# Causal attention with decay and a SiLU feed-forward: score matmuls of two heads in one step, the mask moved from TensorE to VectorE, buffers regrouped

## The chip, the cores and the metric

The kernel runs on one core of a Trainium2 chip. The metric is the device time of one execution in microseconds; the time before is the median of five runs. A core has five engines that work side by side: TensorE (PE; its weight loads are shown apart as PEld), VectorE (DVE), ScalarE (ACT), GpSimd (POOL) and SyncE (SP, which here only issues transfers). Each runs its own instructions strictly in the order in which they were compiled and waits for others by semaphores. Matmuls write to PSUM, which has eight banks of 2 KB per partition; all else lies in SBUF.

## The reference

Eight batches of eight heads, 576 tokens, head size 64; then a feed-forward from 512 to 2048 and back over all 4608 tokens.

```python
scores = scale * np.matmul(q, k.transpose(0, 1, 3, 2))
cum = np.cumsum(np.log(np.clip(f, 0.0001, 1.0)), axis=-1)
scores = np.where(causal, -1e9, scores + cum[..., :, None] - cum[..., None, :])
attn = softmax(scores)                 # over the keys
x = heads_side_by_side(attn @ v)       # (4608, 512)
h = x @ w_in
out = (h * sigmoid(h)) @ w_out         # (4608, 512)
```

## The kernel before

The program is written in Tile: it emits instructions in the order of the Python code, and a scheduler at compile time orders each engine's instructions by that order as priority, taking a later one where an earlier one isn't ready in its own model of time. Buffers come from pools; `bufs` is how many tiles of a tag may live at once, and a tile's slot is given on when its last reader is done.

**A head** (64 in all, `bh` = batch x 8 + head) goes through these steps. The 576 tokens are five blocks, four of 128 and one of 64.

- `load_head` (L155): SP issues three loads (q, k, v) into a staging tile; the last 64 tokens of all heads of a batch come in one load each (`load_tails`, L135) and POOL copies them in.
- `stage_prep` (L173): DVE casts q and k side by side to bf16 (L186, L187), POOL casts v and sets a column of ones beside it (L190 to L197), PE transposes the five blocks into one PSUM tile `tpqk` (L201), DVE copies that to `qkT` (L205): q transposed in partitions 0 to 63, k transposed in 64 to 127. SP then moves k's half to partitions 0 to 63 of `kT` by a transfer (L207), because both operands of a score matmul must lie in the same partitions.
- `stage_scores` (L210): for each block of keys, transposed scores (keys on partitions, queries at or after the block as columns): matmuls of at most 512 columns into `sc` (L223), which is one PSUM bank with two buffers. For the diagonal block a second matmul adds -30000 where the key comes after the query (L232: `tneg` against the identity). ACT takes the exponential with the decay as a bias per partition into `uT` (L239). That is six score matmuls, five mask matmuls and six exponentials a head: 448 + 128, 448, 320, 192 and 64 columns.
- `stage_av` (L258): for each block of queries PE multiplies `uT` by v with its column of ones (L268, fifteen matmuls a head) into one PSUM tile `av` (two buffers); DVE takes the reciprocal of the sums and multiplies (L278, L279; L288, L289 for the last 64 tokens) into `y`.

**A batch** ends with `stage_xT` (L295): twenty transposes through a PSUM tile `tpx` (pool `ptr`, one buffer), copied by DVE (L307) into `xT`.

**The feed-forward** works on nine groups of 512 tokens. `moe_m1` (L316): for each of 16 blocks of the hidden size four matmuls into `hp` (L323), then ACT's tanh (L331) and a gating multiply on DVE that reads `hp` again (L334). `moe_m2` (L344): for each of four blocks of tokens sixteen matmuls into `po` (L352), a scaled copy by ACT (L360) and a store issued by POOL (L363). `hp` and `po` share two PSUM buffers. After a batch m1 of the group that it completes is emitted, then m2 of the group before (`maybe_emit_moe_after_batch`, L378). As later heads come later in the program, they fill the gaps of m1 and run alone when m2 is done. After the last batch two groups' m1 and three groups' m2 are left, with no heads beside them but those at the beginning.

Loads are emitted four heads ahead and preparations two heads ahead (L391, L392). The PSUM banks: `tpqk` 1, `sc` 2, `av` 2, `tpx` 1, `hp` and `po` 2.

Of the kernel before, what the change touches and what calls it, by code (L numbers as in the profile page):

```python
# [8 lines left out]

ACT = mybir.ActivationFunctionType  # L10
ALU = mybir.AluOpType
FP32 = mybir.dt.float32
BF16 = mybir.dt.bfloat16
P = 128

MASK_ON_PE = True


@with_exitstack
def kernel(  # L20
# [46 lines left out]
    if MASK_ON_PE:  # L67
        tneg = const.tile([P, P], BF16, name="tneg")
        make_upper_triangular(nc, tneg, val=-30000.0, diag=False)
    else:  # L70
# [56 lines left out]
    psc = ctx.enter_context(tc.tile_pool(name="psc", bufs=2, space=bass.MemoryType.PSUM))  # L127
    pav = ctx.enter_context(tc.tile_pool(name="pav", bufs=2, space=bass.MemoryType.PSUM))
    ptr = ctx.enter_context(tc.tile_pool(name="ptr", bufs=1, space=bass.MemoryType.PSUM))
    php = ctx.enter_context(tc.tile_pool(name="php", bufs=2, space=bass.MemoryType.PSUM))  # L130

    stg: dict[int, tuple] = {}
# [37 lines left out]
        )  # L170
        stg[bh] = (qkf, vf)

    def stage_prep(bh):  # L173
        b, h = divmod(bh, H)
        qkf, vf = stg[bh]
        if HAS_TAIL:
            qt, kt, vt = tails[b]
            nc.gpsimd.tensor_copy(out=qkf[:NT_TAIL, NB - 1, 0:D], in_=qt[:NT_TAIL, h, :])
            nc.gpsimd.tensor_copy(
                out=qkf[:NT_TAIL, NB - 1, D : 2 * D], in_=kt[:NT_TAIL, h, :]  # L180
            )
            nc.gpsimd.tensor_copy(out=vf[:NT_TAIL, NB - 1, :], in_=vt[:NT_TAIL, h, :])
        qk_bf = conv.tile([P, NB, 2 * D], BF16, name="qk_bf", tag="qk_bf")
        v_bf = conv.tile([P, NB, D + 1], BF16, name="v_bf", tag="v_bf")
        if HAS_TAIL:
            nc.vector.tensor_copy(out=qk_bf[:, 0 : NB - 1, :], in_=qkf[:, 0 : NB - 1, :])  # L186
            nc.vector.tensor_copy(  # L187
                out=qk_bf[:NT_TAIL, NB - 1, :], in_=qkf[:NT_TAIL, NB - 1, :]
            )
            nc.gpsimd.tensor_copy(out=v_bf[:, 0 : NB - 1, 0:D], in_=vf[:, 0 : NB - 1, :])  # L190
            nc.gpsimd.tensor_copy(
                out=v_bf[:NT_TAIL, NB - 1, 0:D], in_=vf[:NT_TAIL, NB - 1, :]
            )
        else:
            nc.vector.tensor_copy(out=qk_bf[:, :, :], in_=qkf[:, :, :])
            nc.gpsimd.tensor_copy(out=v_bf[:, :, 0:D], in_=vf[:, :, :])
        nc.gpsimd.memset(v_bf[:, :, D : D + 1], 1.0)  # L197
        tp = ptp.tile([P, S], BF16, name="tpqk", tag="tpqk")
        for c in range(NB):
            n = bs[c]  # L200
            nc.tensor.transpose(  # L201
                tp[:, c * P : c * P + n], qk_bf[:n, c, :], ident_bf[:n, :n]
            )
        qkT = qktp.tile([P, S], BF16, name="qkT", tag="qkT")
        nc.vector.tensor_copy(out=qkT[:, :], in_=tp[:, :])  # L205
        kT = qktp.tile([P, S], BF16, name="kT", tag="kT")
        nc.sync.dma_start(out=kT[0:D, :], in_=qkT[D : 2 * D, :])  # L207
        return (qkT[0:D, :], kT[0:D, :], v_bf)

    def stage_scores(bh, prepped):  # L210
        b, h = divmod(bh, H)
        qT, kT, v_bf = prepped
        u = upool.tile([P, UW], BF16, name="uT", tag="uT")
        for kb in range(NB):
            nk = bs[kb]
            q0 = kb * P
            nqtot = S - q0
            col = 0
            first = True
            while col < nqtot:  # L220
                ncols = min(448 if (nqtot - col) > 512 else 512, nqtot - col)
                sc = psc.tile([P, 512], FP32, name="sc", tag="sc")
                nc.tensor.matmul(  # L223
                    sc[:nk, 0:ncols],
                    lhsT=kT[:, q0 : q0 + nk],
                    rhs=qT[:, q0 + col : q0 + col + ncols],
                    start=True,
                    stop=(not (first and MASK_ON_PE)),
                )
                if first and MASK_ON_PE:  # L230
                    nq0 = nk
                    nc.tensor.matmul(  # L232
                        sc[:nk, 0:nq0],
                        lhsT=tneg[:nq0, 0:nk],
                        rhs=ident_bf[:nq0, :nq0],
                        start=False,
                        stop=True,
                    )
                nc.scalar.activation(  # L239
                    out=u[:nk, uoff[kb] + col : uoff[kb] + col + ncols],  # L240
                    in_=sc[:nk, 0:ncols],
                    func=ACT.Exp,
                    bias=negcumT[:nk, kb, bh : bh + 1],
                    scale=scale,
                )
                if first and not MASK_ON_PE:
                    nq0 = nk
                    nc.vector.tensor_tensor(
                        out=u[:nk, uoff[kb] : uoff[kb] + nq0],
                        in0=u[:nk, uoff[kb] : uoff[kb] + nq0],  # L250
                        in1=mask01[:nk, :nq0],
                        op=ALU.mult,
                    )
                col += ncols
                first = False
        return (u, v_bf)

    def stage_av(bh, scored):  # L258
        b, h = divmod(bh, H)
# [53 lines left out]
    NG = (NT + TG - 1) // TG  # L313
    gstate: dict[int, tuple] = {}

    def moe_m1(g):  # L316
        t0 = g * TG
        ntg = min(TG, NT - t0)
        gte = gpool.tile([P, NFC, TG], BF16, name="gtile", tag="gtile")
        for fc in range(NFC):  # L320
            hp = php.tile([P, TG], FP32, name="hp", tag="hp")
            for cc in range(NCC):
                nc.tensor.matmul(  # L323
                    hp[:, :ntg],
# [19 lines left out]
    def moe_m2(g):  # L344
# [2 lines left out]
        nb_tok = (ntg + P - 1) // P  # L347
        for tb in range(nb_tok):
            ntb = min(P, ntg - tb * P)
            po = php.tile([P, TG], FP32, name="po", tag="hp")  # L350
            for fc in range(NFC):
                nc.tensor.matmul(  # L352
                    po[:ntb, :DM],
# [34 lines left out]
    ytiles: dict[int, bass.AP] = {}  # L388
    prepped: dict[int, tuple] = {}

    LOAD_AHEAD = 4  # L391
    PREP_AHEAD = 2  # L392

    load_tails(0)
# [5 lines left out]
    ytiles[0] = ypool.tile([P, NB, DM], BF16, name="y", tag="y")  # L400
    for bh in range(min(PREP_AHEAD, BH)):
        pb, _ = divmod(bh, H)
        if pb not in ytiles:
            ytiles[pb] = ypool.tile([P, NB, DM], BF16, name="y", tag="y")
        prepped[bh] = stage_prep(bh)

    for bh in range(BH):
        b, h = divmod(bh, H)
        if b not in ytiles:
            ytiles[b] = ypool.tile([P, NB, DM], BF16, name="y", tag="y")  # L410
        scored = stage_scores(bh, prepped[bh])
        lt = bh + LOAD_AHEAD
        if lt < BH:
            lb, lh = divmod(lt, H)
            if lh == 0 and lb not in tails:
                load_tails(lb)
            load_head(lt)
        nxt = bh + PREP_AHEAD
        if nxt < BH:
            nb2, nh2 = divmod(nxt, H)  # L420
            if nb2 not in ytiles:
                ytiles[nb2] = ypool.tile([P, NB, DM], BF16, name="y", tag="y")
            prepped[nxt] = stage_prep(nxt)
        stage_av(bh, scored)
        if h == H - 1:
            stage_xT(b)
            maybe_emit_moe_after_batch(b)

    for g in range(NG):
        if g not in gstate:  # L430
# [36 lines left out]
```

## Time and profile before

| what | us |
|---|---|
| median of five runs | 608.18 |
| lowest, highest | 607.56, 610.42 |
| the profiled execution | 607.63 |
| its span, first to last instruction | 605.5 |
| mean granted TensorE clock over the span | 0.874 of full |

The costliest kinds of work, by busy time in the span: m1's matmuls 158.7, m2's 125.6, the score matmuls 131.7, the mask matmuls 80.5, the av matmuls 97.5 us on PE; the exponentials 170.7 and tanh 86.1 on ACT; the gating multiply 98.7 on DVE. How to read such lines: an instruction is named by its line in the kernel, its engine, its operation, what it writes and reads, and its shape; behind the bar stand its busy time in all, the mean of one in ns, then how long the engine stood idle before such instructions and what ended that. Matmuls overlap in time, so the sum of their durations exceeds the time that they hold PE; their start times tell what each one costs.

### The profile page before, as it was taken

Reading aid. Unit: us, or ns where it says so; the run is one execution under the profiler, and the core shown is the slowest. Engines: PE = TensorE matmul, PEld = TensorE weight load, DVE = VectorE, ACT = ScalarE, POOL = GpSimd, SP = SyncE. Lnnn points to the kernel's source line nnn. Section 1 sums busy time; section 2 is a strip of 40 time slices with the busy share of each in tenths; the row PEclk is TensorE's granted clock in tenths of the full one; section 3 lists DMA queues with packets and bytes.
Section 4 is the critical chain, followed back from the end, with each engine's and each line's share of the span. In section 5 each row is a group of like instructions: output and inputs, shape, how many; then the busy total and the mean of one; then the engine's idle time right before and its main releaser. Section 6 shows DMA issues by size and latency. Waiting matters only on the chain.

```text
span 605.5 us, 9158 instructions
## 1 busy us (share of the span) xinstructions
PE 548.0 (90%) x3301; PEld 262.3 (43%) x3301; DVE 233.5 (39%) x634; ACT 275.1 (45%) x572; POOL 102.1 (17%) x432
## 2 busy tenths in 40 slices
PE   0039999999999999999999999999999998888896
PEld 0015554454445444544454445544454444333342
DVE  1033345644604461546244633454245502532400
ACT  1025545655626472647354734564355535333311
POOL 2032221222122111311031112100110010001011
PEclk9999999957996699759985998599858995899999
DMA  8993443634674412441243034200100020001011
GB/s 169 204 171 77 102 102 80 144 71 111 154 171 116 105 41 75 121 109 38 61 125 88 19 78 116 51 15 28 62 16 6 11 74 6 1 14 57 1 69 70
DMA packets 124765, 47.41 MB, mean 78 GB/s; under 512 B 115696, under 2 KB 121840, under 8 KB 124720
## 3 DMA queue, kind: packets, MB, share of 16 engines
q1 hardware_dynamic: 119248, 33.20, 25.6%
q0 software_dynamic: 5472, 13.63, 7.9%
q8 instruction: 26, 0.43, 0.3%
q14 instruction: 19, 0.16, 0.1%
HBM read 36.85 MB, written 9.44 MB: 76 GB/s over the span
## 4 chain that ended last, share of the span: by engine, by line
PE 73%; issue 16%; SPq 5%; ACT 2%; DMA 1%; POOL 1%; DVE 1%; POOLq 0%; ACTq 0%; DVEq 0%
PE hp L323 18%; PE sc L223 16%; PE po L352 14%; PE av L268 10%; PE sc L232 7%; PE tpqk L201 5%; PE tpx L302 3%; SPq L163 2%; ACT uT L239 2%; SPq L167 1%; SPq L159 1%; POOL out_dram L363 1%; DMA qkf<-in_k_dram 1%; DMA kT<-qkT 1%; ACT L239 0%
## 5 line engine op out<-in xcount | busy, mean ns | idle before, releaser
L239 ACT ACTIVATE uT<-sc,negcumT 128x448 bf16<-128x448 f32 (+4 forms) x384 | 170.7, 480 | 91.8 <-PE sc L232 88.9
L323 PE MATMUL hp<-xT,w_in_bf 128*128 128x512 bf16 x576 | 158.7, 402 | 6.3 <-DVE gtile L334 5.4
L223 PE MATMUL sc<-qkT,kT 64*128 64x448 bf16 (+4 forms) x384 | 131.7, 346 | 10.1 <-ACT uT L239 6.2
L334 DVE SCALAR_TENSOR_TENSOR gtile<-th,hp 128x512 bf16<-128x512 bf16 x144 | 98.7, 686 | 74.4 <-ACT th L331 73.5
L331 ACT ACTIVATE th<-hp 128x512 bf16<-128x512 f32 x144 | 86.1, 598 | 90.9 <-PE hp L323 73.3
L352 PE MATMUL po<-w_out_bf,gtile 128*128 128x512 bf16 x576 | 125.6, 379 | 0.8 <-DVE gtile L334 0.8
L268 PE MATMUL av<-v_bf,uT 128*128 128x65 bf16 (+2 forms) x960 | 97.5, 225 | 0.1
L352 PEld LDWEIGHTS <-gtile 128*128 128x128 bf16 x576 | 56.0, 98 | 67.7 <-issue 1.3
L268 PEld LDWEIGHTS <-uT 128*128 128x128 bf16 (+2 forms) x960 | 66.8, 118 | 34.0 <-issue 20.2
L232 PE MATMUL sc<-ident_bf,tneg 128*128 128x128 bf16 (+1 forms) x320 | 80.5, 252 | 0.0
L323 PEld LDWEIGHTS <-w_in_bf 128*128 128x128 bf16 x576 | 50.9, 102 | 61.0 <-issue 23.2
L205 DVE COPY qkT<-tpqk 128x576 bf16<-128x576 bf16 x64 | 29.2, 456 | 115.9 <-PE tpqk L201 46.8
L190 POOL CAST v_bf<-vf 128x256 bf16<-128x256 f32 x64 | 25.5, 399 | 269.1 <-PE av L268 154.5
L201 PE MATMUL tpqk<-ident_bf,qk_bf 128*128 128x128 bf16 (+1 forms) x320 | 45.3, 256 | 26.4 <-DVE qk_bf L186 18.4
L360 ACT ACTIVATE osb<-po 128x512 f32<-128x512 f32 x36 | 21.5, 597 | 104.3 <-PE po L352 104.3
L223 PEld LDWEIGHTS <-kT 64*128 64x128 bf16 (+1 forms) x384 | 37.9, 101 | 54.6 <-issue 30.8
L232 PEld LDWEIGHTS <-tneg 128*128 128x128 bf16 (+1 forms) x320 | 34.5, 108 | 57.2 <-issue 47.2
L363 POOL DMA_DIRECT2D out_dram<-osb x36 | 19.5, 542 | 167.5 <-ACT osb L360 164.6
L201 PEld LDWEIGHTS <-qk_bf 128*128 128x128 bf16 (+1 forms) x320 | 26.1, 112 | 41.7 <-DVE qk_bf L186 18.6
L186 DVE CAST qk_bf<-qkf 128x512 bf16<-128x512 f32 x64 | 27.2, 424 | 39.1 <-DMA qkf<-in_k_dram 27.8
L278 DVE RECIPROCAL rec<-av 128x4 f32<-128x4 f32 x64 | 11.7, 183 | 77.2 <-PE av L268 76.3
L279 DVE TENSOR_TENSOR y<-av,rec 128x256 bf16<-128x256 f32 x64 | 27.1, 424 | 2.0
(31 smaller groups left out, 177.4 us busy)
## 6 DMA issues: line engine op xcount, KB each, us to landing
out_dram<-osb POOLq DMA_DIRECT2D x36, 256.0 KB, 2.3
qkf<-in_q_dram SPq DMA_DIRECT2D x64, 128.0 KB, 2.8
qkf<-in_k_dram SPq DMA_DIRECT2D x64, 128.0 KB, 2.9
vf<-in_v_dram SPq DMA_DIRECT2D x64, 128.0 KB, 2.5
kT<-qkT SPq DMA_DIRECT2D x64, 72.0 KB, 2.0
w_in_bf<-in_moe_w_in_dram POOLq DMA_DIRECT2D x1, 2048.0 KB, 13.8
w_out_bf<-in_moe_w_out_dram POOLq DMA_DIRECT2D x1, 2048.0 KB, 26.1
qt<-in_q_dram SPq DMA_DIRECT2D x8, 128.0 KB, 3.2
```

The lines of the kernel that those rows point to most:

```text
L186: nc.vector.tensor_copy(out=qk_bf[:, 0 : NB - 1, :], in_=qkf[:, 0 : NB - 1, :])
L201: nc.tensor.transpose(tp[:, c * P : c * P + n], qk_bf[:n, c, :], ident_bf[:n, :n])
L205: nc.vector.tensor_copy(out=qkT[:, :], in_=tp[:, :])
L223: nc.tensor.matmul(sc[:nk, 0:ncols], lhsT=kT[:, q0 : q0 + nk], rhs=qT[:, q0 + col : q0 + col + ncols], start=True, stop=(not (first and MA ...
L232: nc.tensor.matmul(sc[:nk, 0:nq0], lhsT=tneg[:nq0, 0:nk], rhs=ident_bf[:nq0, :nq0], start=False, stop=True,)
L239: nc.scalar.activation(out=u[:nk, uoff[kb] + col : uoff[kb] + col + ncols], in_=sc[:nk, 0:ncols], func=ACT.Exp, bias=negcumT[:nk, kb, bh : ...
L268: nc.tensor.matmul(av[:nq, qb, :], lhsT=u[:nk, loff : loff + nq], rhs=v_bf[:nk, kb, 0 : D + 1], start=(kb == 0), stop=(kb == qb),)
L279: nc.vector.tensor_tensor(out=y[:, 0:nfull, h * D : (h + 1) * D], in0=av[:, 0:nfull, 0:D], in1=rec[:, 0:nfull, None].to_broadcast([P, nful ...
L323: nc.tensor.matmul(hp[:, :ntg], lhsT=w_in_bf[:, cc, fc * P : (fc + 1) * P], rhs=xT[:, cc, t0 : t0 + ntg], start=(cc == 0), stop=(cc == NCC ...
L331: nc.scalar.activation(out=th[:, :ntg], in_=hp[:, :ntg], func=ACT.Tanh, scale=0.5)
L334: nc.vector.scalar_tensor_tensor(out=gte[:, fc, :ntg], in0=th[:, :ntg], scalar=1.0, in1=hp[:, :ntg], op0=ALU.add, op1=ALU.mult,)
L352: nc.tensor.matmul(po[:ntb, :DM], lhsT=gte[:, fc, tb * P : tb * P + ntb], rhs=w_out_bf[:, fc, :], start=(fc == 0), stop=(fc == NFC - 1),)
```

## The change

Scores are computed for two heads at once (`PAIR_SCORES`). Of a pair, the even head has q and k in partitions 0 to 63 as before; for the odd head the transfer moves q up, so that q and k lie in partitions 64 to 127. A tile `sc` now has two banks (still two buffers), one bank per head; the two score matmuls are emitted one behind the other under `tc.high_priority()`, which gives them the priority of the program's start. Then come the two heads' exponentials.

The mask matmul is gone. After the exponential of a diagonal block DVE overwrites with zeros what lies below the diagonal of that transposed block, where the key comes after the query (`copy_predicated` with a mask of int16).

To make room in PSUM, `av` has one buffer in place of two and `tpx` takes its slot from the same tag. The pools `conv`, `qktp` and `upool` grow by one, `stage` shrinks from 12 to 10. Loads are emitted six heads ahead, preparations one pair ahead. After the last head, every second output tile of m1 and m2 takes a slot of `sc`, so that four buffers take turns in place of two.

```diff
-MASK_ON_PE = True
+MASK_MODE = "pred"
+PAIR_SCORES = True
...
+        mask_lo = const.tile([P, P], mybir.dt.int16, name="mask_lo")
+        make_lower_triangular(nc, mask_lo, val=1.0, diag=False)
+        zeros = const.tile([P, P], BF16, name="zeros")
+        nc.gpsimd.memset(zeros[:, :], 0.0)
...
-    stage = ctx.enter_context(tc.tile_pool(name="stage", bufs=12))
+    stage = ctx.enter_context(tc.tile_pool(name="stage", bufs=10))
     tailp = ctx.enter_context(tc.tile_pool(name="tailp", bufs=2))
-    conv = ctx.enter_context(tc.tile_pool(name="conv", bufs=3))
-    qktp = ctx.enter_context(tc.tile_pool(name="qktp", bufs=3))
-    upool = ctx.enter_context(tc.tile_pool(name="upool", bufs=2))
+    conv = ctx.enter_context(tc.tile_pool(name="conv", bufs=4))
+    qktp = ctx.enter_context(tc.tile_pool(name="qktp", bufs=4))
+    upool = ctx.enter_context(tc.tile_pool(name="upool", bufs=3))
...
-    pav = ctx.enter_context(tc.tile_pool(name="pav", bufs=2, space=bass.MemoryType.PSUM))
-    ptr = ctx.enter_context(tc.tile_pool(name="ptr", bufs=1, space=bass.MemoryType.PSUM))
+    pav = ctx.enter_context(tc.tile_pool(name="pav", bufs=1, space=bass.MemoryType.PSUM))
...
+        sh = qktp.tile([P, S], BF16, name="shT", tag="shT")
+        if upper:
+            nc.sync.dma_start(out=sh[D : 2 * D, :], in_=qkT[0:D, :])
+            return (sh[D : 2 * D, :], qkT[D : 2 * D, :], v_bf)
+        else:
+            nc.sync.dma_start(out=sh[0:D, :], in_=qkT[D : 2 * D, :])
+            return (qkT[0:D, :], sh[0:D, :], v_bf)
...
+            nc.vector.copy_predicated(
+                out=u[:nk, col_off : col_off + nq0],
+                mask=mask_lo[:nk, :nq0],
+                data=zeros[:nk, :nq0],
+            )
...
+                sc = psc.tile([P, 2, 512], FP32, name="sc", tag="sc")
+                with tc.high_priority():
+                    for i, bh in enumerate(bhs):
+                        qT, kT, v_bf = preps[i]
+                        nc.tensor.matmul(
+                            sc[:nk, i, 0:ncols],
+                            lhsT=kT[:, q0 : q0 + nk],
+                            rhs=qT[:, q0 + col : q0 + col + ncols],
+                            start=True,
+                            stop=(not (first and MASK_MODE == "matmul")),
+                        )
+                for i, bh in enumerate(bhs):
+                    nc.scalar.activation(
+                        out=us[i][:nk, uoff[kb] + col : uoff[kb] + col + ncols],
+                        in_=sc[:nk, i, 0:ncols],
+                        func=ACT.Exp,
+                        bias=negcumT[:nk, kb, bh : bh + 1],
+                        scale=scale,
                     )
...
+                    if first and MASK_MODE != "matmul":
+                        apply_mask(us[i], nk, nk, uoff[kb])
...
-            tp = ptr.tile([P, NCC, P], BF16, name="tpx", tag="tpx")
+            tp = pav.tile([P, NCC, P], BF16, name="tpx", tag="av")
...
+    def moe_psum(nm):
+        if not tailflag[0]:
+            return php.tile([P, TG], FP32, name=nm, tag="hp")
+        tailn[0] += 1
+        if tailn[0] % 2:
+            return php.tile([P, TG], FP32, name=nm, tag="hp")
+        t2 = psc.tile([P, 2, 512], FP32, name="sc", tag="sc")
+        return t2[:, 0, :]
...
+    for gi, grp in enumerate(groups):
+        b0 = grp[0] // H
+        for bh in grp:
+            ensure_y(bh // H)
+        scored = stage_scores(list(grp), [prepped[bh] for bh in grp])
+        for bh in grp:
+            lt = bh + LOAD_AHEAD
...
+        if gi + 1 < len(groups):
+            for bh in groups[gi + 1]:
+                ensure_y(bh // H)
+                prepped[bh] = stage_prep(bh, is_upper(bh))
+        for i, bh in enumerate(grp):
+            b, h = divmod(bh, H)
+            stage_av(bh, scored[i])
+            if h == H - 1:
+                stage_xT(b)
+                tailflag[0] = bh == BH - 1
+                maybe_emit_moe_after_batch(b)
```

More of the change, by code (lines that the diff above doesn't have):

```diff
@@ L7 @@
 from concourse._compat import with_exitstack
-from concourse.masks import make_identity, make_upper_triangular
+from concourse.masks import (
+    make_identity,
+    make_lower_triangular,
+    make_upper_triangular,
+)
 ACT = mybir.ActivationFunctionType
@@ L221, in stage_scores @@
                 ncols = min(448 if (nqtot - col) > 512 else 512, nqtot - col)
[L222 to L237, printed above, removed]
-                    )
@@ L239, in stage_scores @@
[L239 to L253, printed above, removed]
+                sc = psc.tile([P, 2, 512], FP32, name="sc", tag="sc")
@@ L254, in stage_scores @@
                 col += ncols
                 first = False
-        return (u, v_bf)
+        return [(us[i], preps[i][2]) for i in range(len(bhs))]
     def stage_av(bh, scored):
@@ L314 @@
     gstate: dict[int, tuple] = {}
+    tailflag = [False]
+    tailn = [0]
+    def moe_psum(nm):
[6 more added lines that the diff above has]
+        return t2[:, 0, :]
     def moe_m1(g):
@@ L389, with is_upper, ensure_y @@
     prepped: dict[int, tuple] = {}
-    LOAD_AHEAD = 4
-    PREP_AHEAD = 2
-    load_tails(0)
+    LOAD_AHEAD = 6
+    if PAIR_SCORES:
+        groups = [(bh, bh + 1) if bh + 1 < BH else (bh,) for bh in range(0, BH, 2)]
+    else:
+        groups = [(bh,) for bh in range(BH)]
+    def is_upper(bh):
+        return PAIR_SCORES and (bh % 2 == 1)
+    def ensure_y(b):
+        if b not in ytiles:
+            ytiles[b] = ypool.tile([P, NB, DM], BF16, name="y", tag="y")
     for bh in range(min(LOAD_AHEAD, BH)):
```

74 lines of the change are left out of this document (34 added, 40 removed).

## The prediction

> **What bounds the kernel now.** I read the busy times first, then the span by stages, then the order of TensorE's work in one head.
>
> ```profile
> PE 548.0 (90%) x3301; PEld 262.3 (43%) x3301; DVE 233.5 (39%) x634; ACT 275.1 (45%) x572; POOL 102.1 (17%) x432
> ```
>
> TensorE (PE) is the only engine near full; VectorE (DVE) and ScalarE (ACT) are under half. But the span is made of unlike stages, so next come stretches of it (columns: stretch, its length, then busy us and count of instructions for PE, PEld, DVE, ACT and POOL, then the granted clock, DMA share, GB/s):
>
> ```profile
> 42.60:90.00 47.40, 46.60 (x304) 24.47 (x304) 18.09 (x64) 26.40 (x59) 10.90 (x51) 1.00 0.40 89
> 305.40:328.70 23.30, 22.89 (x174) 12.67 (x173) 11.03 (x40) 13.93 (x31) 7.23 (x33) 0.65 0.47 113
> 328.70:333.20 4.50, 4.50 (x22) 1.70 (x20) 1.74 (x4) 0.60 (x1) 0.00 (x0) 0.52 0.33 75
> 328.70:354.00 25.30, 25.30 (x154) 11.17 (x152) 15.61 (x36) 14.71 (x30) 3.20 (x16) 0.92 0.20 46
> 354.00:367.90 13.90, 13.90 (x68) 6.17 (x65) 0.69 (x1) 2.88 (x6) 1.82 (x5) 1.00 0.24 77
> 517.70:538.80 21.10, 18.43 (x79) 7.25 (x77) 11.72 (x19) 9.16 (x16) 0.00 (x0) 0.93 0.00 1
> 552.60:572.10 19.50, 15.41 (x66) 6.17 (x65) 10.32 (x15) 10.05 (x17) 0.54 (x1) 1.00 0.04 14
> ```
>
> The first row is the opening run of heads; the next four are one round, which recurs seven times: attention heads alone (23.3 us), the first MoE product m1 with heads in its gaps (25.3, its first 4.5 shown apart), the second product m2 alone (13.9). The last two rows are m1 in the tail, with no heads left. In the round PE is busy 98 to 100%: every nanosecond of PE work there is on the path. In the last row it is busy 15.41 of 19.50, for 64 matmuls of the size and number that m2 does in 13.9. How many heads a stage holds is the count of L288, once per head (here columns are DVE alone):
>
> ```profile
> 305.40:328.70 23.30, 0.74 (x5) 0.65 0.47 113
> 328.70:354.00 25.30, 0.45 (x3) 0.92 0.20 46
> ```
>
> Five heads take 4.66 us each alone, three hide in m1. Now one head on PE, by start times, at a low clock:
>
> ```profile
> 192.02 0.55 PE L223 MATMUL sc<-qkT,kT 64*128 64x448 bf16 x1
> 192.50 0.26 PE L268 MATMUL av<-v_bf,uT 64*64 64x65 bf16 x1
> 192.69 0.29 PE L232 MATMUL sc<-ident_bf,tneg 128*128 128x128 bf16 x1
> 192.91 0.28 PE L223 MATMUL sc<-qkT,kT 64*128 64x128 bf16 x1
> 193.13 0.77 PE L201 MATMUL tpqk<-ident_bf,qk_bf 128*128 128x128 bf16 x5
> 193.76 0.53 PE L223 MATMUL sc<-qkT,kT 64*128 64x448 bf16 x1
> 194.22 0.29 PE L232 MATMUL sc<-ident_bf,tneg 128*128 128x128 bf16 x1
> 194.45 0.45 PE L223 MATMUL sc<-qkT,kT 64*128 64x320 bf16 x1
> 194.82 0.29 PE L232 MATMUL sc<-ident_bf,tneg 128*128 128x128 bf16 x1
> 194.91 0.32 PE L268 MATMUL av<-v_bf,uT 128*128 128x65 bf16 x2
> 195.24 0.32 PE L223 MATMUL sc<-qkT,kT 64*128 64x192 bf16 x1
> 195.48 0.29 PE L232 MATMUL sc<-ident_bf,tneg 128*128 128x128 bf16 x1
> 195.57 0.37 PE L268 MATMUL av<-v_bf,uT 128*128 128x65 bf16 x3
> 195.87 0.26 PE L223 MATMUL sc<-qkT,kT 64*64 64x64 bf16 x1
> 195.94 0.24 PE L232 MATMUL sc<-ident_bf,tneg 64*64 64x64 bf16 x1
> 196.12 0.82 PE L268 MATMUL av<-v_bf,uT 128*128 128x65 bf16 x9
> 196.87 0.55 PE L223 MATMUL sc<-qkT,kT 64*128 64x448 bf16 x1
> ```
>
> From one 448-column score to the next head's is 4.85 us, without a wait. Durations overlap, so each step is priced by the start of the next. The five masks (L232) take 0.22 + 0.23 + 0.09 + 0.09 + 0.18 = 0.81. A mask that a 64-row score follows takes 0.23; one that a 128-row av matmul follows takes 0.09: part of the price is the change of shape. The six scores (L223) take 0.48 + 0.22 + 0.46 + 0.37 + 0.24 + 0.07 = 1.84.
>
> **The change part by part.** *Masks leave PE:* 0.81 us a head at this clock. At full clock the same pair of steps shows
>
> ```profile
> 371.08 0.23 PE L232 MATMUL sc<-ident_bf,tneg 128*128 128x128 bf16 x1
> 371.24 0.31 PE L223 MATMUL sc<-qkT,kT 64*128 64x320 bf16 x1
> ```
>
> that is 0.16 for 0.23, a ratio of 0.70, so I take 0.57 there.
>
> *Scores in pairs:* head 2k has q and k on rows 0 to 63, head 2k+1 on rows 64 to 127, each with its own PSUM bank. No row shows both halves at once. The pair's steps cost between one head's 1.84 (both halves together) and twice that (one after the other): a saving of 0.92 to 0 a head, at full clock 0.64 to 0. I take the whole saving, since the rows say that a score uses 64 of the rows and the other head's operands lie on the other 64. Less than nothing is excluded: the matmuls are the same and the changes of shape become fewer. The Trainium skill, "TensorEngine Tiling (Array Packing)", Key Properties, says that tiles work independently and that a change of tiling mode drains the engine; the mask rows' 0.23 against 0.09 agree with the drain, and nothing here tests the independence. By its first half alone the forecast below holds; without it the first rival does.
>
> So a head needs 4.85 - 0.81 - 0.92 = 3.1 us of PE at the low clock.
>
> *Masks land on DVE:* five predicated copies a head, 128 or 64 elements a row, inputs in SBUF. None is in the trace. The nearest rows:
>
> ```profile
> L279 DVE TENSOR_TENSOR y<-av,rec 128x256 bf16<-128x256 f32 x64 | 27.1, 424 | 2.0
> L289 DVE TENSOR_SCALAR y<-av,rec 64x64 bf16<-64x64 f32 x64 | 17.4, 272 | 1.1
> L187 DVE CAST qk_bf<-qkf 64x128 bf16<-64x128 f32 x64 | 13.9, 218 | 0.2 <-POOL qkf L179 0.2
> ```
>
> 218 ns is one input of the same length, 424 two inputs at twice the length. I take 0.26, nearer to the first, since length counts for most; 5 x 0.26 = 1.3 us a head, with ends of 1.1 and 2.1. Over 64 heads DVE goes from 233.5 to some 317 us busy. In the lone heads DVE works 11.03 / 5 = 2.2 us a head, then 3.5. ACT is unchanged:
>
> ```profile
> L239 ACT ACTIVATE uT<-sc,negcumT 128x448 bf16<-128x448 f32 (+4 forms) x384 | 170.7, 480 | 91.8 <-PE sc L232 88.9
> ```
>
> six exponentials of 480 ns, 2.9 us a head. So in the lone stretch the order turns round: DVE 3.5, PE 3.1, ACT 2.9. Each mask also waits for its exponential, and the av matmuls of its block for it; what queues behind on DVE is the next heads' casts, the copies to qkT, and in m1 the gating multiply that frees the hp buffers. Three engines so close don't interlock perfectly: I allow DVE 92%, 3.8 us a head (an estimate).
>
> *One av buffer for two, shared with tpx:* the second head's av must wait until DVE has read the first's. The read is L279 and L289 (0.70) with two reciprocals ahead, about 1.0. Cover: PE meanwhile has the next pair's scores, emitted at high priority, and its tpqk transposes. If that cover is gone it is the second rival. The deeper conv, qktp and uT pools hold two heads at once, the 12 to 10 stage buffers still hold six heads ahead: nothing.
>
> *Start:* the first pair needs two transfers (one a head, as before) ahead of its first exponentials of both heads; SP issues them in its queue:
>
> ```profile
> 36.69 0.52 SPq L207 DMA_DIRECT2D kT<-qkT  x1
> 37.26 0.59 SPq L159 DMA_DIRECT2D qkf<-in_q_dram  x1
> 37.95 0.51 SPq L207 DMA_DIRECT2D kT<-qkT  x1
> ```
>
> The second is 1.26 later: +1.3 us, once. Loading six heads ahead in place of four puts no more before them: SP already put loads of a later head between the two. POOL's two more constants are single short operations.
>
> *Tail:* output tiles of m1 and m2 after the last head come from four buffers, not two. The 552.60 stretch should shrink from 19.5 to near m2's 13.9; I take 14.8, -4.7. In the 517.70 stretch I take PE's idle time, 21.10 - 18.43 = 2.7.
>
> *Sum.* Lone heads of a round: 5 x (4.66 - 3.8) = -4.3. m1 stretch: PE loses 3 x (0.57 + 0.64) = 3.6 of 25.3; DVE there is 15.61 + 3 x 1.3 = 19.5 in 21.7, 90%, so I give back 0.8: -2.8. m2 stays. Seven rounds of -7.1: -49.7. The opening stretch, 47.4 us for nine heads, is at the slow pace (its clock is printed 1.00, but 5.3 us a head isn't): 9 x (4.85 - 3.8) = -9.5. Tail -7.4, start +1.3. Together -65.3. The profiled execution took 607.6 (span 605.5 and 2.1 around it), 0.6 under the median: 608.2 - 65.3 = 543 us.
>
> **The rivals.** *The halves don't run together.* Then only the masks are saved: lone heads 0.75 each (between 0.57 and 0.81, clock 0.65), 3.8 a round; m1 3 x 0.57 = 1.7; seven rounds 38.5, opening 9 x 0.81 = 7.3, tail 7.4, start +1.3: 556 us. For it: no row shows two halves at work. Against it: the two write separate banks and read separate rows.
>
> *The single av buffer becomes a chain.* If the next pair's exponentials can't start until the av results of this one are out, a pair takes 2 x 2.9 of exponentials, then the first head's last nine av matmuls (0.75), their reading (1.0), the second head's fifteen (0.33 + 0.30 + 0.75 + 0.19 = 1.6), their reading (1.0): 10.1, or 5.05 a head. Against 4.66 that is +1.9 a round in the lone stretch with nothing gained in m1, opening +1.8, tail -7.4, start +1.3: 608.2 + 9, 617 us. It decides from about 4.8 us a head, where 44 lone heads eat the tail's gain. Against it: uT has three buffers, so one head of the next pair can go on, and nine of fifteen av matmuls need not wait for the end.
>
> *The clock stays low in m1.* The lone heads run at 0.65 and m1 starts at 0.52 over its first 4.5 us, then recovers (0.92 over the stretch). If a PE that idles more never recovers, m1's matmuls take twice 13.9, with three heads of 3.1 some 37 us for 22.5: +14.6 x 7 on 543, 645 us; it turns to a loss from 9 us a round. Against it: 64 long matmuls a stretch stay, and they raised the clock each time. The Trainium skill, "TensorE: Matmul & The Clock Gate", Part 1, says that the clock halves after idle windows and returns after about 3.4 us of sustained work; the 4.5 us above agree.
>
> *Better overlap:* DVE full at 3.3 a head (masks at 218 ns) and m1 losing all 3.6: 10.4 a round, opening 14, tail and start as above: 515 us.
>
> **How the numbers follow.** Forecast, with the better overlap in it, 0.62; halves apart 0.20; av chain 0.10; low clock 0.04; mixed effects that cancel 0.04. A difference under 0.3% (1.8 us) can't be told from none here. Faster 0.84, same 0.04, slower 0.12. The range goes from 512, just under the better overlap, to 575, past the halves-apart case with DVE waits of its own; above lie the chain and the clock.
>
> **What would show it.** Right: PE's busy time near 450, DVE's near 317; two score matmuls of a pair starting within some tens of ns; lone heads at 3.8 with DVE the fullest; predicated copies near 0.26; the last m1 at 14.8. Wrong: predicated copies above 0.42; PE waiting for reciprocals or L289 before av for microseconds; m1 stretches at a clock near 0.5.

## The result and the profile after

The changed kernel takes 529.84 us (median of nine; 526.86 to 531.06) against 608.5 (median of sixteen): a ratio of 0.869, 95% interval 0.868 to 0.871. The forecast was 543 with a range of 512 to 575: faster, and by 13 us more than said. The busy times of the profiled execution (span 526.6 us):

```profile
PE 447.8 (85%) x2981; PEld 220.6 (42%) x2981; DVE 287.5 (55%) x954; ACT 256.6 (49%) x572; POOL 107.9 (20%) x433
```

PE fell by 100 us, to the 450 that was forecast. DVE rose by 54 and not by the 84 that was forecast, though the copies themselves cost what was forecast (below): the durations of all DVE instructions add up to 253 us before and 339 after, 86 more, but busy time counts a moment once where instructions overlap. The same kinds of stretch as before, in the same columns: the opening, one round (heads alone, m1, m2), and the two m1 of the tail:

```profile
44.20:84.90 40.70, 31.68 (x250) 18.17 (x250) 27.75 (x113) 24.87 (x63) 12.62 (x54) 1.00 0.61 134
220.30:235.00 14.70, 11.39 (x116) 7.13 (x116) 12.08 (x52) 9.37 (x24) 6.13 (x25) 0.77 0.62 145
235.00:259.20 24.20, 24.20 (x176) 11.35 (x174) 18.71 (x59) 17.14 (x39) 4.14 (x20) 0.93 0.30 68
259.20:273.50 14.30, 14.30 (x70) 6.33 (x69) 1.55 (x5) 2.39 (x4) 2.03 (x5) 1.00 0.25 80
448.50:465.70 17.20, 17.20 (x79) 7.77 (x78) 11.26 (x19) 8.96 (x15) 0.00 (x0) 0.85 0.00 0
479.40:493.40 14.00, 14.00 (x67) 6.34 (x66) 9.88 (x15) 9.57 (x17) 0.54 (x1) 1.00 0.05 19
```

The heads that end in the lone stretch and in m1, again by one DVE instruction a head (now L309):

```profile
220.30:235.00 14.70, 0.59 (x4) 0.77 0.62 145
235.00:259.20 24.20, 0.60 (x4) 0.93 0.30 68
```

Two things are to be seen. A lone head now takes 14.7 / 4 = 3.7 us in this round (forecast 3.8). And m1, as long as before, holds four heads where it held three, so fewer are left to run alone. The lone stretch shrank from 23.3 to 14.7, twice what I had forecast. In it no engine is full any more: PE 11.4 of 14.7, DVE 12.1.

To compare kernels I cut every span at three places: the first exponential, the beginning of m1 of the first group, and that of m1 of the eighth (the last but one); m1's beginning is taken 1.1 us ahead of the group's first tanh. "Half clock" is the time at which the records grant PE half its clock; the records show only full and half, and none exists for the opening, so it is left out there.

| kernel | median us | until the first exponential | opening | middle | tail | half clock |
|---|---|---|---|---|---|---|
| before | 608.5 | 42.6 | 48.1 | 428.2 | 86.5 | 153 |
| changed | 529.8 | 44.2 | 41.5 | 364.0 | 76.9 | 87 |
| same_half | 545.5 | 44.3 | 45.5 | 377.3 | 75.5 | 95 |
| mask_on_pe | 549.1 | 44.2 | 45.4 | 380.6 | 77.3 | 97 |
| no_prio | 539.4 | 44.3 | 41.5 | 375.1 | 77.2 | 125 |
| tail_two | 540.0 | 43.7 | 41.5 | 365.1 | 87.1 | 90 |
| before_mask_dve | 554.3 | 43.6 | 43.6 | 379.5 | 86.5 | 105 |
| before_tail_four | 599.0 | 43.1 | 48.1 | 429.4 | 75.8 | 160 |
| single_heads | 567.5 | 42.9 | 44.8 | 401.8 | 76.5 | 125 |
| four_undone | 593.5 | 44.2 | 47.9 | 413.3 | 86.5 | 144 |
| before_av_one | 618.1 | 42.7 | 48.2 | 438.4 | 86.5 | 177 |
| mask_pool | 527.3 | 44.3 | 42.8 | 362.7 | 76.4 | 87 |
| late_weights | 522.9 | 22.6 | 57.2 | 365.0 | 76.6 | 91 |
| pool_late | 511.6 | 19.9 | 54.1 | 359.8 | 75.5 | 85 |

One of the four runs of mask_on_pe took 829 us and one of the four of tail_two 803, in a slower state; the medians given include them, and those of the other three runs are 548.9 and 539.9.

In the profiles of all kernels but before, changed and pool_late, 39 to 41 of the 1152 feed-forward matmuls have no record (PE x2940 beside PEld x2981), so PE's busy time there reads about 4 us too low. That is an estimate, with each missing one put in behind its weight load.

Between the first two rows the start costs 1.6, the opening gains 6.6, the middle 64.2 and the tail 9.6: 78.8 us of span. The forecast had, for the same four, a cost of 1.3 and gains of 9.5, 49.7 and 7.4. The surplus lies in the middle. The middle as seven rounds, m1 and m2 each from the first to the last of its weight loads and the lone stretch between m2 and the next m1 ("exps" are exponentials):

| kernel | lone stretches, us | heads that end there | m1, us | heads that end there | exps in m1 | exps in m2 |
|---|---|---|---|---|---|---|
| before | 175.7 | 35 | 165.0 | 18 | 100 | 8 |
| changed | 100.9 | 25 | 171.3 | 29 | 164 | 28 |
| no_prio | 135.3 | 29 | 154.0 | 23 | 101 | 12 |
| before_mask_dve | 123.3 | 27 | 168.7 | 25 | 139 | 5 |
| mask_pool | 109.0 | 28 | 165.2 | 24 | 148 | 12 |

Over all rounds a lone head takes 175.7 / 35 = 5.0 us before and 100.9 / 25 = 4.0 after, so the round shown is one of the shorter ones.

### The profile page after: what moved, and what is told of

It reads as the page before. It is cut to its first block, busy times and chain, and to the rows that moved or that the text cites. A ratio compares the mean times of both kernels' runs of the same rounds, so it can differ in the third digit from the quotient of the medians.

```text
span 526.6 us, 8852 instructions
## 1 busy us (share of the span) xinstructions
PE 447.8 (85%) x2981; PEld 220.6 (42%) x2981; DVE 287.5 (55%) x954; ACT 256.6 (49%) x572; POOL 107.9 (20%) x433
## 4 chain that ended last, share of the span: by engine, by line
PE 57%; issue 20%; SPq 7%; DVE 6%; DMA 4%; ACT 3%; POOL 2%; POOLq 0%; ACTq 0%; DVEq 0%
PE hp L356 20%; PE po L385 13%; PE av L289 9%; PE sc L258 8%; PE tpqk L213 4%; PE tpx L323 3%; SPq L175 3%; ACT uT L266 2%; SPq L179 2%; SPq L171 2%; DMA qkf<-in_k_dram 2%; POOL out_dram L396 2%; DVE qkT L217 1%; DMA shT<-qkT 1%; DVE y L300 1%
## 5 line engine op out<-in xcount | busy, mean ns | idle before, releaser
L266 ACT ACTIVATE uT<-sc,negcumT 128x448 bf16<-128x448 f32 (+4 forms) x384 | 157.2, 490 | 57.7 <-PE sc L258 55.3
L356 PE MATMUL hp<-xT,w_in_bf 128*128 128x512 bf16 x512 | 146.8, 407 | 1.9 <-DVE gtile L367 1.7
L364 ACT ACTIVATE th<-hp 128x512 bf16<-128x512 f32 x128 | 77.2, 603 | 67.0 <-PE hp L356 61.7
L385 PE MATMUL po<-w_out_bf,gtile 128*128 128x512 bf16 x480 | 107.8, 379 | 0.0
L235 DVE COPY_PREDICATED uT<-mask_lo,zeros 128x128 bf16<-128x128 int16 (+1 forms) x320 | 80.1, 273 | 27.4 <-ACT uT L266 24.9
L289 PE MATMUL av<-v_bf,uT 128*128 128x65 bf16 (+2 forms) x960 | 72.7, 209 | 11.1 <-DVE uT L235 7.4
L356 PEld LDWEIGHTS <-w_in_bf 128*128 128x128 bf16 x576 | 51.1, 102 | 57.2 <-issue 16.9
L289 PEld LDWEIGHTS <-uT 128*128 128x128 bf16 (+2 forms) x960 | 54.7, 108 | 46.7 <-issue 14.6
L258 PE MATMUL sc<-qkT,shT 64*128 64x448 bf16 (+1 forms) x192 | 55.5, 328 | 7.8 <-ACT uT L266 5.7
L258 PE MATMUL sc<-shT,qkT 64*128 64x448 bf16 (+2 forms) x192 | 56.2, 337 | 2.9 <-DMA shT<-qkT 2.9
L258 PEld LDWEIGHTS <-shT 64*128 64x128 bf16 x192 | 16.1, 101 | 34.4 <-issue 28.6
L190 POOL COPY qkf<-qt 64x64 f32<-64x64 f32 x64 | 17.3, 272 | 47.8 <-DVE qk_bf L199 40.4
```

Source lines behind the costliest of these rows:

```text
L235: nc.vector.copy_predicated(out=u[:nk, col_off : col_off + nq0], mask=mask_lo[:nk, :nq0], data=zeros[:nk, :nq0],)
L258: nc.tensor.matmul(sc[:nk, i, 0:ncols], lhsT=kT[:, q0 : q0 + nk], rhs=qT[:, q0 + col : q0 + col + ncols], start=True, stop=(not (first and ...
L266: nc.scalar.activation(out=us[i][:nk, uoff[kb] + col : uoff[kb] + col + ncols], in_=sc[:nk, i, 0:ncols], func=ACT.Exp, bias=negcumT[:nk, k ...
L289: nc.tensor.matmul(av[:nq, qb, :], lhsT=u[:nk, loff : loff + nq], rhs=v_bf[:nk, kb, 0 : D + 1], start=(kb == 0), stop=(kb == qb),)
L356: nc.tensor.matmul(hp[:, :ntg], lhsT=w_in_bf[:, cc, fc * P : (fc + 1) * P], rhs=xT[:, cc, t0 : t0 + ntg], start=(cc == 0), stop=(cc == NCC ...
L364: nc.scalar.activation(out=th[:, :ntg], in_=hp[:, :ntg], func=ACT.Tanh, scale=0.5)
```

## The experiments

The theory after the result: PE was the bound, and four parts each took work or waits from it: masks moved, halves together, scores early, buffers in the tail. The rival: one part did nearly everything, and DVE, with 80 us of masks, now sets the pace. The first four runs undo one part each in the changed kernel.

**same_half: both heads of a pair on rows 0 to 63.**

```diff
     def is_upper(bh):
-        return PAIR_SCORES and (bh % 2 == 1)
+        return False
```

> The changed kernel with both heads of a pair on rows 0 to 63: same matmuls, same pairs, but the two halves can't run together. If PE is still what bounds the changed kernel, the scores take 0.6 to 0.9 us a head more of it and most of that shows: 545 to 570 us against 529.8. If VectorE and its masks now set the pace and PE's gain lay idle, it stays within 3 us of 530. My prediction's price for this case was 13 us.

545.48 us, ratio to before 0.896 (0.894 to 0.899): 15.6 us slower than the change, so the halves together are worth that. The start times show them. In the changed kernel (PE, start, duration), two pairs of scores, 448 and 320 columns:

```profile
279.98 0.55 PE L258 MATMUL sc<-qkT,shT 64*128 64x448 bf16 x1
279.99 0.55 PE L258 MATMUL sc<-shT,qkT 64*128 64x448 bf16 x1
280.46 0.42 PE L258 MATMUL sc<-qkT,shT 64*128 64x320 bf16 x1
280.47 0.44 PE L258 MATMUL sc<-shT,qkT 64*128 64x320 bf16 x1
```

and the same four on one half, merged by the view into one row:

```profile
291.39 1.46 PE L258 MATMUL sc<-qkT,shT 64*128 64x448 bf16 x4
```

The second of a pair starts 10 ns behind the first, and the four are through in 0.93 us (279.98 to 280.47 + 0.44) against 1.46; both places are at half clock. But PE's busy time is only 16.5 us higher on one half, some 20 with the missing records:

```profile
PE 464.3 (86%) x2940; PEld 228.9 (42%) x2981; DVE 289.5 (53%) x954; ACT 259.2 (48%) x572; POOL 108.1 (20%) x433
```

That is 0.26 to 0.31 us a head, where the forecast priced the whole saving at 0.64 to 0.92. The forecast's price was taken from one score to the start of the next step, against single heads. The same price over the whole trace (averaged for each number of columns where PE didn't stand idle behind the score, summed over a head's six) parts it:

| six scores of a head, us | full clock | half clock |
|---|---|---|
| before | 1.19 | 1.87 |
| single_heads (below) | 1.19 | 1.86 |
| same_half: pairs on one half | 0.92 | 1.57 |
| changed: pairs on both halves | 0.68 | 0.94 |

Pairs save 0.51 and 0.93 us a head in all, near the forecast at half clock and under its 0.64 at full. Of this the second half gives 0.24 and 0.63; the rest, 0.27 and 0.30, comes from the order alone, two scores of one shape side by side.

**mask_on_pe: the mask again as a matmul, in the pair order.**

```diff
+                    if first and MASK_MODE == "matmul":
+                        for i, bh in enumerate(bhs):
+                            nc.tensor.matmul(
+                                sc[:nk, i, 0:nk],
+                                lhsT=tneg[:, 0:nk],
+                                rhs=ident_bf[:, :nk],
+                                start=False,
+                                stop=True,
+                            )
```

(with `MASK_MODE = "matmul"`, so that no predicated copy is left.)

> The changed kernel with the mask again as a matmul into each bank (over all 128 rows, also for the 64-token block) and no predicated copies. If PE binds: 0.57 to 0.81 us a head come back on it, 550 to 575 us, though VectorE falls by some 80 us of busy time. If VectorE's masks are the bound: no slower than 530, perhaps 520. PE granted clock should rise a little in the lone heads in neither case.

549.05 us, 0.899 (0.894 to 0.904): 19.2 us slower, just under the span expected for a PE that binds, and far from the rival.

**no_prio: score matmuls in program order.**

```diff
-                with tc.high_priority():
+                if True:
```

> The changed kernel with the score matmuls in plain program order. If the rounds came out shorter than forecast because scores at the program's start priority run inside m2 and early in m1, so that their exponentials are done there: 537 to 550 us, and no scores inside the m2 stretches. If the order is the same without it: 528 to 532.

539.37 us, 0.886 (0.884 to 0.888): 9.5 us slower, all of it in the middle. A round of this kernel, heads alone and then m1, four heads ending in each:

```profile
223.80:243.70 19.90, 17.87 (x147) 10.17 (x147) 16.32 (x67) 12.19 (x31) 7.41 (x29) 0.63 0.53 127
243.70:264.90 21.20, 20.98 (x144) 9.64 (x145) 16.38 (x47) 14.80 (x31) 4.38 (x20) 0.95 0.40 91
```

The lone stretch is 5 us longer and its clock 0.63 for 0.77; m1 is 3 us shorter. ACT's exponentials within one m2 stretch of the changed kernel, and then of this one:

```profile
372.80:388.60 15.80, 4.65 (x12) 1.00 0.16 56
```

```profile
380.00:394.00 14.00, 1.94 (x6) 1.00 0.24 84
```

So the early scores do move exponentials into m2, in some rounds a whole pair's twelve. In this round four heads end in m1 with and without the priority; over the seven rounds it is 29 with and 23 without, and 25 against 29 in the lone stretches.

**tail_two: two buffers in the tail.**

```diff
-                tailflag[0] = bh == BH - 1
+                tailflag[0] = False
```

> The changed kernel with two output buffers in the tail as before. If the two waits on freed buffers were the whole tail gain: 529.8 + 7 to 10, 537 to 540 us, and the last m1 at 19 us for 14. If other things limit it: within 2 us of 530.

540.02 us, 0.886 (0.884 to 0.888): 10.2 us slower, all in the tail, and the last m1 is at 19.1 us again (484.4 to 503.5).

The second group turns it round: one part alone in the kernel before, and more taken out of the changed one.

**before_mask_dve: the kernel before, masks on DVE.**

```diff
-MASK_ON_PE = True
+MASK_ON_PE = False
...
-                    nc.vector.tensor_tensor(
+                    nc.vector.copy_predicated(
                         out=u[:nk, uoff[kb] : uoff[kb] + nq0],
-                        in0=u[:nk, uoff[kb] : uoff[kb] + nq0],
-                        in1=mask01[:nk, :nq0],
-                        op=ALU.mult,
+                        mask=mask_lo[:nk, :nq0],
+                        data=zeros[:nk, :nq0],
                     )
```

> The kernel before with one part of the change alone: mask matmuls replaced by predicated copies on VectorE. If the masks cost PE what the start times say (0.57 to 0.81 us a head) and VectorE hides the copies: 608.4 - 64 x 0.7 = 564 us, within 557 to 572. If the copies, waiting for their exponentials, hold up VectorE's queue and with it PE in this one-head-at-a-time order: 585 us or more.

554.32 us, 0.910 (0.907 to 0.912): 54.8 us faster than its own runs of before (609.12), more than expected. This part alone makes two thirds of the gain, though undoing it costs 19.2. The busy times tell much of why. Of this kernel, and then of mask_on_pe:

```profile
PE 491.0 (89%) x2941; PEld 233.2 (42%) x2981; DVE 291.1 (53%) x954; ACT 273.7 (49%) x572; POOL 108.2 (20%) x433
```

```profile
PE 470.5 (86%) x3260; PEld 244.3 (45%) x3301; DVE 227.6 (42%) x634; ACT 260.0 (47%) x572; POOL 107.1 (20%) x432
```

With heads one by one the same 320 masks hold PE for 548.0 - 491.0 = 57 us; in pairs for 470.5 - 447.8 = 23. With the missing records it is some 53 and 27, and the clock changes along with the masks. At a given clock the start times say the same: a head's five masks cost 0.59 us at full and 0.83 at half clock in the kernel before, 0.31 and 0.55 in mask_on_pe. That two masks side by side share a change of shape, which one mask between two scores has to itself, fits this; it was not tested apart from the priority, and four_undone (below), with pairs but without priority, stands between at 0.45 and 0.64.

**before_tail_four: the kernel before, four buffers in the tail.**

```diff
-            hp = php.tile([P, TG], FP32, name="hp", tag="hp")
+            hp = moe_psum("hp")
...
-            po = php.tile([P, TG], FP32, name="po", tag="hp")
+            po = moe_psum("po")
...
+        if tailn[0] % 2:
+            return php.tile([P, TG], FP32, name=nm, tag="hp")
+        return psc.tile([P, 512], FP32, name="sc", tag="sc")
...
+            tailflag[0] = bh == BH - 1
```

> The kernel before with four output buffers in the tail alone (hp and the one-bank sc in turn). Undoing it in the changed kernel cost 10.2 us. If the tail is a stage by itself: 608.4 - 10 = 598 us, 597 to 600. If it works only with the rest of the change: over 603.

598.95 us, 0.983 (0.980 to 0.986): 10.2 us faster than its own before (609.12), as much as undoing it cost. The tail is a stage by itself.

**single_heads: pairs off in the changed kernel.**

```diff
-PAIR_SCORES = True
+PAIR_SCORES = False
```

> The changed kernel with pairs off: one head at a time (all on rows 0 to 63), preparation one head ahead, everything else as changed. Against the run with pairs on one half (545.5 us) it tells what emitting two heads' scores, masks and exponentials side by side is worth without the halves running together. If that order matters (fewer changes of shape on PE, work at hand while one head waits): 555 to 575. If pairing is only a means to use both halves: 543 to 548.

567.45 us, 0.932 (0.929 to 0.935): 22 us slower than pairs on one half. By time the pair order is worth more than the halves: PE is busy 494.7 us for 464.3. It is not the changes of shape alone: the score matmuls wait 15.4 us for exponentials here and 5.2 in same_half. It is also slower than masks and tail alone would make the kernel before (554.3 - 10.2 = 544). What else it has is one av buffer and one preparation ahead.

**four_undone: the first four runs' edits together.** (Both heads on one half, mask on PE, no priority, two buffers in the tail; pairs, pools and loads six ahead stay.)

> The changed kernel with the four parts undone together that cost 15.6, 19.2, 9.5 and 10.2 us one by one: both heads on one half, mask on PE, no priority, two buffers in the tail. What is left of the change is pairs, buffer counts and loads six ahead. If the parts add up: 529.8 + 54.5 = 584 us. If parts shared a gain (a PE that is nowhere full pays for none of them alone): 595 to 608, and what is left is worth little.

593.46 us, 0.974 (0.970 to 0.977), between the two expectations: undone together the four cost 63.6 where one by one they cost 54.5. They add up roughly, each being worth a little more where the others are missing. What is left, 15.7 us under its own before (609.12), is the pair order with its pools and the deeper loading; no run parts these.

**before_av_one: the kernel before with one av buffer.**

```diff
-    pav = ctx.enter_context(tc.tile_pool(name="pav", bufs=2, space=bass.MemoryType.PSUM))
-    ptr = ctx.enter_context(tc.tile_pool(name="ptr", bufs=1, space=bass.MemoryType.PSUM))
+    pav = ctx.enter_context(tc.tile_pool(name="pav", bufs=1, space=bass.MemoryType.PSUM))
...
-            tp = ptr.tile([P, NCC, P], BF16, name="tpx", tag="tpx")
+            tp = pav.tile([P, NCC, P], BF16, name="tpx", tag="av")
```

> The kernel before with one av buffer, tpx in the same slot, as in the change, and nothing else. The changed kernel with pairs off (567.5 us) is slower than mask and tail alone would give (554.3 - 10.2 = 544). If the single buffer is what costs those 23 us when heads come one by one: 608.4 + 15 to 30, 623 to 640 us, with PE waiting for VectorE's reading of av. If the one preparation ahead (in place of two) is: 607 to 613.

618.06 us, 1.014 (1.012 to 1.017): 8.3 us slower than its own before (609.80), between the expectations. The loss lies in the middle, with 24 us more at half clock. It isn't the wait that was expected: no wait of the av matmuls for DVE's reading shows in the trace, and PE is busy 5.6 us longer (some 9 with the missing records). How one buffer lengthens the middle stays open. If it costs as much in single_heads, it is a third of the 23 us that are lacking there; the rest may be the shorter preparation, which wasn't tried.

The last three ask what bounds the changed kernel, and whether it can be beaten.

**mask_pool: the masks on GpSimd.**

```diff
-            nc.vector.copy_predicated(
-                out=u[:nk, col_off : col_off + nq0],
-                mask=mask_lo[:nk, :nq0],
-                data=zeros[:nk, :nq0],
-            )
+            nc.gpsimd.affine_select(
+                out=u[:nk, col_off : col_off + nq0],
+                in_=u[:nk, col_off : col_off + nq0],
+                compare_op=ALU.is_ge,
+                fill=0.0,
+                base=0,
+                pattern=[[1, nq0]],
+                channel_multiplier=-1,
+            )
```

> The changed kernel with the zeros below the diagonal set by GpSimd (affine select on uT) in place of VectorE's predicated copies. If VectorE sets the pace of lone heads, as forecast (3.5 us a head of its work against 3.1 of PE): lone heads fall towards PE's pace and the time to 505 to 522 us. If VectorE's copies lie beside other work: 526 to 534. If GpSimd's queue (casts of v, copies of the tails) makes the mask late: over 535.

527.33 us, 0.865 (0.863 to 0.867): 2.5 us faster than the change, with runs that overlap (526.1 to 528.0 against 526.9 to 531.1). DVE loses 56 us of busy time and it hardly shows:

```profile
PE 440.7 (84%) x2940; PEld 221.8 (42%) x2981; DVE 231.8 (44%) x634; ACT 257.6 (49%) x572; POOL 188.4 (36%) x753
```

A lone stretch of it, again with four heads:

```profile
225.00:243.20 18.20, 13.87 (x130) 8.37 (x127) 11.23 (x37) 10.26 (x25) 11.98 (x49) 0.66 0.52 125
```

No engine is over 77% busy in it, and over the seven rounds a lone head takes 109.0 / 28 = 3.9 us for 4.0. So DVE's load doesn't bind the lone heads. The run isn't clean, though: the scheduler arranged the heads differently (24 end in m1 for 29), and PE and its weight loads wait 23.4 us in all for GpSimd's masks where they waited 18.6 for DVE's. What remains is the chain from score through exponential and mask to av, the loads (in the chain that ended last one transfer of v stands for 2.1 us of this stretch, for 2.6 of the 14.7 in the changed kernel), and a PE at 0.66 of its clock; no run parts these.

**late_weights: both weight loads held back.** A one-element copy from a head's staged v into the weight tile makes the load behind it wait.

```diff
+    nc.gpsimd.tensor_copy(out=w_in_bf[0:1, 0, 0:1], in_=stg[3][1][0:1, 0, 0:1])
     nc.gpsimd.dma_start(
         out=w_in_bf[:, :, :], in_=moe_w_in.rearrange("(cc p) f -> p cc f", p=P)
     )
+    nc.gpsimd.tensor_copy(out=w_out_bf[0:1, 0, 0:1], in_=stg[5][1][0:1, 0, 0:1])
     nc.gpsimd.dma_start(
         out=w_out_bf[:, :, :], in_=moe_w_out.rearrange("(fc p) m -> p fc m", p=P)
     )
```

> The changed kernel with the two weight loads held back until the loads of heads 3 and 5 have landed. It tells whether the first 44 us before the first exponential are transfers that the weights crowd out. If so the first exponential moves from 44 to 15 to 22 us and the time to 500 to 510. If the heads' own loads set that start: 520 to 530.

522.94 us, 0.858 (0.856 to 0.860). The first exponential came at 22.6 us, and yet only 7 us were won: the opening grew by 16. SP's queue shows where it went (start, duration, issue):

```profile
17.22 8.38 SPq L165 DMA_DIRECT2D qkf<-in_q_dram  x1
25.64 0.51 SPq L169 DMA_DIRECT2D qkf<-in_k_dram  x1
26.20 6.49 SPq L173 DMA_DIRECT2D vf<-in_v_dram  x1
32.78 3.26 SPq L217 DMA_DIRECT2D shT<-qkT  x1
```

An issue that takes 0.5 us elsewhere stands for 8 and 6 us while the weights land (issued at 14.1 and 17.6, landed at 28.2 and 41.6), and with it the transfers to shT behind it.

**pool_late: masks on GpSimd, weights later still.** (w_in after the loads of head 7, w_out after those of head 11, in the same manner, on top of mask_pool.)

> The changed kernel with the masks on GpSimd (it measured 527.3 us) and the weights held back further than in the run before (522.9): w_in until the loads of head 7 have landed, w_out until those of head 11. In that run the first exponential came at 22.6 us, but SyncE's queue then stood 8 and 6 us behind the weights, and the opening run of heads grew by 16 us. If the weights' transfers are what stands in the way there: the opening shrinks and the time is 508 to 518 us. If heads at the low clock or the loads themselves set the opening: 519 to 523, the two small gains added.

511.62 us, 0.841 (0.839 to 0.844): it beats both kernels, the changed one by 18 us. Start and opening together take 74.0 us, 13 less than in mask_pool. One load still stands 6.7 us in SP's queue:

```profile
32.12 6.74 SPq L165 DMA_DIRECT2D qkf<-in_q_dram  x1
```

## Why the prediction was right, and where it was off

*PE bounds; work taken from it shows:* right. PE's busy time fell by 100 us and the span by 79.

*Masks on PE at 0.57 to 0.81 us a head:* as a price by start times it held, 0.59 and 0.83 over the whole trace. The time gained is larger. Taken out alone they gave 54.8 us, 0.86 a head over 64, and 48.7 in the middle, 0.89 a head over the 55 heads after the opening. In the opening, which has no clock record, they gave only 4.5 for nine heads, 0.5 a head. In the middle the clock changes too: half-clock time fell from 153 to 105 us. Half clock begins 5.1 to 9.9 us after the start of each lone stretch before, so a shorter stretch has less of it; and 25 heads for 18 end in m1, which runs at 0.89 to 0.95 of the clock. That this makes up the whole difference is argued from the tables; no run changed the clock alone.

*Halves together, 0.64 to 0.92 a head:* the mechanism was right and the size at half clock too, 0.93, but the halves give only 0.63 of that, and 0.24 of 0.51 at full clock; the rest is the order, which I had not set apart. By the result the halves are worth 15.6 us. My rival without them stood 13 us above the forecast; that closeness is partly luck, since it left out what pairs save on one half, and since PE no longer binds the lone heads.

*Masks on DVE at 0.26 us:* right, 0.273 on the average:

```profile
L235 DVE COPY_PREDICATED uT<-mask_lo,zeros 128x128 bf16<-128x128 int16 (+1 forms) x320 | 80.1, 273 | 27.4 <-ACT uT L266 24.9
```

*DVE then paces lone heads, 3.5 us and an allowance to 3.8:* the number came out, 3.7 in the round shown and 4.0 over all, and the reason fell. Part of it is luck: 129 exponentials lie in the lone stretches, where 25 whole heads have 150, so some of their work is done in m1 and m2. DVE is the fullest there, 12.1 of 14.7 us, but taking the masks off it gave 2.5 us, not the 8 to 25 that a binding DVE would have given.

*Heads stay where they are, five alone and three in m1:* this step failed. m1 didn't shrink, it took in more heads: 29 for 18 over the seven rounds, and 25 for 35 are left alone. I left out of the sum that scores at the program's start priority move exponentials into m2 and m1 and heads into m1; I named the priority only as cover for the av buffer. Undoing it costs 9.5 us, the nearest that a run comes to the surplus of 13. It isn't the only cause: masks on DVE alone bring 25 heads into m1 without any priority.

*One av buffer as cover's price:* in the pair order no chain formed; av matmuls wait 3.4 us in all for DVE's reading. In the old order the buffer costs 8.3 us, though not by that wait. What a second buffer would bring in the pair order wasn't tried.

*The clock stays low in m1:* it did not; m1 stands at 0.93 as against 0.92, and over the span half-clock time fell to 87 us. Nor was it idle time of PE that lowered the clock before. The lone stretch of the round shown in the prediction falls into a part at full clock and one at half clock, and PE is busy nearly throughout both:

```profile
304.80:312.50 7.70, 7.33 (x66) 4.12 (x65) 4.21 (x16) 5.01 (x11) 3.42 (x15) 1.00 0.46 122
312.50:328.60 16.10, 16.07 (x113) 8.76 (x113) 6.83 (x24) 8.91 (x21) 3.81 (x18) 0.50 0.47 105
```

What lowers it is not known from these runs.

*Opening 9.5:* it gained 6.6. PE is busy 31.7 of its 40.7 us, so other things limit it; pool_late shows the weight loads to be one.

*Tail 7.4 and start 1.3:* 9.6 and 1.6. The last m1 gained 5.5 for 4.7. In the first tail m1 I had taken PE's idle time alone, 2.7, and 21.1 us became 17.2; that part of its busy time was waiting too is likely and not shown.

## What to carry to other kernels

Price a short matmul by the start of the next one, but ask which part of that price belongs to the instruction and which to the change of shape around it: the second part seems to be paid once for a group here, so an order that puts like matmuls side by side saves it. Where stages with different limits follow each other, ask what the scheduler will move between them; priority on the operation that feeds an idle engine fills the dense stage. And an engine that is the fullest in a stretch isn't its bound until taking work from it shortens the stretch.

## What the runs showed of the hardware that was not expected

A head's five mask matmuls cost PE 0.59 us at full clock with heads one by one and 0.31 in pairs, start to start (0.83 and 0.55 at half clock). Two scores on the two halves of the rows started within 10 ns of each other, and two such pairs took 0.93 us against 1.46 on one half. Half clock came while PE was busy by the profile for 16.07 of 16.10 us. The time at half clock moved with every edit of the middle, from 177 us (before_av_one) to 85 (pool_late), though no edit aimed at it; it is long where the lone stretches are long (153 us with 175.7 before, 87 with 100.9 after). At the start an issue on SP's queue stood for up to 8.4 us while two weight loads of 2 MB were landing; holding them back brought the first exponential from 44 to 20 us.
